# Sliding-window attention and two MoE-style layers on one core: weight blocks converted in another order

## The chip, the core and the metric

The kernel runs on one core of one Trainium2 chip. The metric is the device time of one execution in microseconds (us). Five engines work side by side, each through its own instructions in order: TensorE (PE in the profile, its weight loads PEld), VectorE (DVE), ScalarE (ACT), GpSimd (POOL) and SyncE (SP), which here only issues the DMA transfers.

## What is computed

```python
x = attention(q, k, v)                 # 2 x 8 heads x 768 x 64, own window of 96 keys and 8 global keys
x = x.transpose(0, 2, 1, 3).reshape(1536, 512)
h = x @ w_in1                          # 512 x 2048
x = (max(h, 0) + alpha * min(h, 0)) @ w_out1
h = x @ w_in2
g = (a0 + a1*h + a2*h*h + a3*h*h*h) / (1 + |b0|*|h| + |b1|*h*h + 1e-6)
out = g @ w_out2                       # 1536 x 512, float32
```

q, k, v are float32; the four weight matrices and the coefficients arrive as float64.

## The kernel before

**Layers.** Each of the two layers works on three groups of 512 tokens (g = 0, 1, 2) and sixteen blocks of 128 inner units (fc or j = 0 to 15). A *step* is one group with one block: `first` (L663) multiplies the block of w_in with the group's x into a bank, `leaky` (layer one) or `rational_a` to `rational_h` (layer two) apply the activation, and `second` (L723) multiplies the result with the block of w_out and adds into banks 4 to 7, which hold the group's four sums of 128 tokens. Every operand is kept as a float32 high half and a low half (hi, lo), so each product is three: 12 matmuls of 128x512 in `first`, 12 in `second`.

**Order of the steps.** `plan_weights` (L214) writes the list of 96 steps by hand. Layer one: group 0, then 1, then 2 with the lower blocks 0 to 7 (steps 0 to 23), then the groups 0, 1, 2 with the upper blocks 8 to 15 (24 to 47). Layer two: the same, lower blocks in steps 48 to 71, upper ones in 72 to 95. So every group's sum is in two parts: after the lower blocks `drain` (L748) copies the four banks to `part` (or `first`) and saves them to DRAM, `fetch` (L771) brings them back, and after the upper blocks `drain` adds them to the banks on VectorE (L763). In layer one ScalarE then writes the new high half of x (L768) and VectorE, a little later, the low half (L769).

**Slots.** Slot s issues `first(s)`, the activation of step s-1 and `second(s-2)`. Slots 0 to 15 (`joint_slot`) stand beside attention: each also carries two of its 48 pieces (`half`, `before`), and there `second` is one slot nearer. From slot 16 (LATE) on, `plain_slot` (L812) has the layers alone. Every slot calls `tick` twice, so half-slots are numbered 2s and 2s+1.

**Conversion of weights.** 64 jobs (two layers, sixteen blocks, "in" and "out") each turn 128x512 float64 values into hi and lo. A job goes through `tick` (L266) in three half-slots: SP has loaded the doubles into one of four `stage` tiles; ScalarE scales the upper word into `de` (L303); in the next half-slot VectorE joins the bits in three passes (L290, L291, L292) into `dx`, after which SP may load the next stage; in the one after that ScalarE casts the high half (L278) and VectorE subtracts it for the low half (L281). That subtraction is put into the list of the next job's three passes at the third place, in the same half-slot as the cast:

```python
        if split:
            self.join.insert(min(2, len(self.join)), split)
```

The half-slot in which a job starts is a table of numbers. Before, the eight lower blocks of layer one start in half-slots -10 to 12, beside attention; the sixteen jobs of the upper ones in 33 to 55 and the 32 of layer two in 57 to 126, two of every three half-slots up to 96 and then every sixth.

**Where blocks live.** Beside attention there is room for four blocks (`early`); the lower eight go through these four slots, are spilled to DRAM (`spill`, L202, the pair of DMAs of a job at L206) and reloaded (`reload`, L211). When attention is done its memory becomes twelve further slots, so that all sixteen blocks have one. SP issues everything in program order: tokens, weights, spills, reloads, saved sums and output; one that waits holds all behind it.

## Time and profile before

| | |
|---|---|
| three runs | 703.98 us median (702.05 to 704.06) |
| the profiled execution | 702.31 us, span 700.4 us |
| busy in the span | PE 653.3, PEld 509.9, DVE 542.2, ACT 379.4, POOL 226.2 us |
| matmuls | 3250 records in the trace |
| DMA | 78.62 MB, mean 112 GB/s |

The span runs from the first to the last instruction; the rest of an execution's time lies around it. Busy time is that of one engine; a matmul's end is modelled, so the starts of products tell more than their durations. A row of a timeline has its start and its duration in us, the engine, the line, and in brackets the idle time ahead of it with what ended it.

### The profile page before, as it was taken

To read this page: it belongs to the slowest core of one execution; us is meant where nothing else is said; L and a number is where in the kernel's file an instruction comes from. 1 tells how busy PE (TensorE), PEld (TensorE's weight loads), DVE (VectorE), ACT (ScalarE), POOL (GpSimd) and SP (SyncE) were. 2 spreads that over 40 slices of the span, in tenths; PEclk is the share of its full clock that TensorE was granted. 3 is DMA by queue.
4 is the path that set the end of the run, shared out by engine and by line. 5 is a ranking of instruction groups with operands and counts; after the bars stand their busy time and mean duration, and the time that the engine had idled before them with its cause. 6 is when DMAs were issued, how large, how long until landed. Compare 5 with 4: busy or idle time off the path is not lost. (4 is left out here: it accounts for less than half of the span.)

```text
span 700.4 us, 9637 instructions
## 1 busy us (share of the span) xinstructions
PE 653.3 (93%) x3250; PEld 509.9 (73%) x3250; DVE 542.2 (77%) x980; ACT 379.4 (54%) x775; POOL 226.2 (32%) x327
## 2 busy tenths in 40 slices
PE   7988898999999999998898996999999999999995
PEld 6656666767777886776676774887878888888784
DVE  4787888634324888889888889999998788797885
ACT  3876565454433334333334237677777676576662
POOL 4785474445442222211112121222212222132221
PEclk8999899999999999999999998999999999999999
DMA  8996778734335435453353151013010030120301
GB/s 164 199 230 180 241 242 249 190 128 124 99 126 178 145 114 172 129 180 90 117 162 113 44 167 59 32 30 91 0 61 1 0 121 0 46 76 0 121 0 65
DMA packets 82554, 78.62 MB, mean 112 GB/s; under 512 B 45056, under 2 KB 61696, under 8 KB 82496
## 3 DMA queue, kind: packets, MB, share of 16 engines
q1 hardware_dynamic: 82496, 77.92, 38.1%
q8 instruction: 27, 0.44, 0.3%
q14 instruction: 31, 0.25, 0.1%
HBM read 58.11 MB, written 17.83 MB: 108 GB/s over the span
## 5 line engine op out<-in xcount | busy, mean ns | idle before, releaser
L679 POOL TENSOR_TENSOR glo<-act,ghi 128x512 fp32r<-128x512 f32 x48 | 64.8, 1349 | 215.0 <-ACT ghi L678 215.0
L721 POOL TENSOR_TENSOR glo<-act,ghi 128x512 fp32r<-128x512 f32 (+1 forms) x49 | 63.7, 1300 | 206.5 <-ACT ghi L717 188.5
L678 ACT CAST ghi<-act 128x512 fp32r<-128x512 f32 x48 | 29.8, 620 | 142.5 <-DVE act L677 131.4
L670 PE MATMUL bank<-xhi,winhi_f 128*128 128x512 f32 x256 | 68.4, 389 | 0.0
L670 PE MATMUL bank<-xhi,winlo_f 128*128 128x512 f32 x256 | 68.4, 389 | 0.0
L670 PE MATMUL bank<-xlo,winhi_f 128*128 128x512 f32 x256 | 68.4, 389 | 0.0
L676 DVE TENSOR_SCALAR act<-bank,al 128x512 f32<-128x512 f32 x48 | 35.8, 746 | 28.7 <-PE bank L670 28.7
L292 DVE SCALAR_TENSOR_TENSOR dx<-stage,dx 128x512 int32<-128x512 int32 x64 | 56.1, 876 | 1.1
L422 ACT ACTIVATE prob<-prob,stat 128x232 f32<-128x232 f32 (+1 forms) x96 | 44.8, 470 | 20.8 <-DVE stat L415 18.5
L670 PEld LDWEIGHTS bank<-xhi,winhi_f 128*128 128x128 f32 x256 | 48.1, 188 | 10.0
L670 PEld LDWEIGHTS bank<-xhi,winlo_f 128*128 128x128 f32 x256 | 48.1, 188 | 10.0
L670 PEld LDWEIGHTS bank<-xlo,winhi_f 128*128 128x128 f32 x256 | 48.1, 188 | 10.0
L434 POOL TENSOR_SCALAR prob<-prob,rec 128x232 f32<-128x232 f32 (+1 forms) x96 | 47.5, 506 | 18.5 <-DVE rec L429 14.7
L688 ACT ACTIVATE stage<-bank 128x512 f32<-128x512 f32 (+1 forms) x49 | 28.8, 588 | 40.2 <-PE bank L670 40.1
L291 DVE SCALAR_TENSOR_TENSOR dx<-de,dx 128x512 int32<-128x512 int32 x64 | 48.6, 759 | 2.2
L736 PE MATMUL bank<-ghi,wouthi_f 128*128 128x512 f32 x112 | 37.1, 422 | 12.7 <-ACT ghi L678 7.5
L415 DVE CUSTOM_DVE_ANT_0 prob<-bank,bm 128x232 f32<-128x232 f32 (+1 forms) x96 | 32.5, 374 | 19.5 <-PE bank L406 19.5
L717 ACT CAST ghi<-act 128x512 fp32r<-128x512 f32 (+1 forms) x49 | 30.2, 616 | 32.1 <-DVE act L714 32.1
L697 DVE SCALAR_TENSOR_TENSOR stage<-stage,abs_b 128x512 f32<-128x512 f32 (+1 forms) x49 | 36.1, 737 | 14.0 <-ACT stage L689 14.0
L736 PE MATMUL bank<-wouthi_f,ghi 128*128 128x512 f32 x144 | 42.2, 394 | 0.8 <-ACT ghi L717 0.8
L303 ACT ACTIVATE de<-stage 128x512 f32<-128x512 f32 x64 | 42.1, 670 | 1.1 <-DMA stage<-in_moe_w_out_dram 1.1
L736 PE MATMUL bank<-wouthi_f,glo 128*128 128x512 f32 x144 | 41.8, 392 | 0.8 <-POOL glo L721 0.7
(202 smaller groups left out, 1540.5 us busy)
## 6 DMA issues: line engine op xcount, KB each, us to landing
stage<-in_moe_w_in_dram SPq DMA_DIRECT2D x32, 512.0 KB, 4.3
stage<-in_moe_w_out_dram SPq DMA_DIRECT2D x32, 512.0 KB, 3.9
part<-saved_f SPq DMA_DIRECT2D x24, 256.0 KB, 4.3
saved_f<-part SPq DMA_DIRECT2D x20, 256.0 KB, 2.5
va<-in_v_dram SPq DMA_DIRECT2D x13, 256.0 KB, 5.9
out_dram<-part SPq DMA_DIRECT2D x11, 256.0 KB
rawk<-in_k_dram SPq DMA_DIRECT2D x10, 256.0 KB, 5.2
rawq<-in_q_dram SPq DMA_DIRECT2D x10, 256.0 KB, 5.7
```

What stands on the lines that cost most here:

```text
L291: lambda: nc.vector.scalar_tensor_tensor(y, e, -(2**31), y, ALU.bitwise_and, ALU.bitwise_or),
L292: lambda: nc.vector.scalar_tensor_tensor(y, low, 29, y, ALU.logical_shift_right, ALU.bitwise_or),
L303: nc.scalar.mul(self.de[n % 2], self.staged(n)[:, :, :, 1].bitcast(F32), 2.0**-112)
L415: nc.vector.tensor_tensor_reduce(p[:, j, :w], banks[pair[j]][:, :w], bm[:, 2 * c + j, :], 1.0, 3.0e38, ALU.add, ALU.min, st[:, j : j + 1])
L422: nc.scalar.activation(p[:, j, :w], p[:, j, :w], AF.Exp, bias=st[:, j : j + 1], scale=-1.0, accum_out=st[:, 2 + j : 3 + j])
L434: nc.gpsimd.tensor_scalar(p[:, j, :w], p[:, j, :w], r[:, j : j + 1], 1.0, ALU.mult, ALU.mult)
L670: nc.tensor.matmul(bk, w["in", a][:, c, :], x[:, c, :], start=e == 0, stop=e == len(seq) - 1)
L676: nc.vector.tensor_scalar(t, h, 0.0, self.al[:, fc : fc + 1], ALU.min, ALU.mult)
L679: nc.gpsimd.tensor_tensor(lo, t, hi.bitcast(F32), ALU.subtract)
L697: nc.vector.scalar_tensor_tensor(w, w, self.ab[:, 0:1], ab, ALU.add, ALU.mult)
L721: nc.gpsimd.tensor_tensor(lo, u, hi.bitcast(F32), ALU.subtract)
L736: nc.tensor.matmul(y[d], lhs, rhs, start=begin and e == 0, stop=last and e == 2)
```

## The change

In layer one group 2, and in layer two group 1, now take all sixteen blocks in one run, so that their sums are never saved, fetched or added; layer one's order becomes 0, 1 (lower), 2 (all), 0, 1 (upper), layer two's 2, 0 (lower), 1 (all), 2, 0 (upper). `drain` then casts group 2's high half straight from the bank and subtracts right behind it. The table of starts changes: the sixteen jobs of layer one's upper blocks start in every second half-slot from 15 to 45; the 32 of layer two in 24 half-slots of 48 to 93 (48, 50, 52, 54, 55, 56, 58, 60, 62, 68, 70, 71, 72, 74, 76, 78, 83, 84, 86, 87, 89, 90, 92, 93) and in eight from 101 to 136, five apart. The jobs of blocks 8 to 11, which start beside attention, have no slot yet: their halves go to `part[1]` and `part[2]`, are spilled from there, and come back by `reload` in slots 18 to 21. The low half's subtraction is kept in a list of its own and issued at the start of the next `tick`. `spill` is called in every `tick` that casts. `fetch` looks one step further ahead.

```diff
@@ tables
+KEPT = CH + 4
+SAVED = ((0, 0), (0, 1), (1, 2), (1, 0))
...
@@ arm
-            self.spilled = [self.alloc_slot(spill, i, "d") for i in range(CH)]
+            self.spilled = [self.alloc_slot(spill, i, "d") for i in range(KEPT)]
...
@@ spill
         while self.unspilled:
-            fc, kind, slot = self.unspilled.popleft()
-            for part in PARTS:
-                self.nc.sync.dma_start(out=words(self.spilled[fc][kind, part]), in_=words(self.slots[slot][kind, part]))
+            to, of = self.unspilled.popleft()
+            self.nc.sync.dma_start(out=to, in_=of)
@@ plan_weights
-        self.steps += [(0, 2, fc, fc) for fc in range(CH)]
-        self.steps += [(0, g, fc, fc) for g in range(NGR) for fc in range(CH, NF)]
-        self.steps += [(1, g, j, j) for half in range(2) for g in range(NGR) for j in range(half * CH, (half + 1) * CH)]
+        self.steps += [(0, 2, fc, fc) for fc in range(NF)]
+        self.steps += [(0, g, fc, fc) for g in (0, 1) for fc in range(CH, NF)]
+        self.steps += [(1, g, j, j) for g in (2, 0) for j in range(CH)]
+        self.steps += [(1, 1, j, j) for j in range(NF)]
+        self.steps += [(1, g, j, j) for g in (2, 0) for j in range(CH, NF)]
...
+        spare = [(fc, kind) for fc in range(CH, NF) for kind in ("in", "out")]
+        for t, (fc, kind) in enumerate(spare):
+            jobs[2 * (CH + t) - 1] = 0, fc, kind, None if fc < KEPT else fc
...
-        times = [t for t in range(2 * LATE, 2 * layer) if t % 3 < 2] + list(range(2 * layer, 2 * (layer + half), 6))
+        times = [t for t in range(48, 96) if (t % 2 == 0 or t in (55, 71) or t > 82) and t not in (64, 66, 80, 82, 85, 88, 91, 94, 95)]
+        times += range(101, 160, 5)
@@ tick
+        while self.splits:
+            self.splits.popleft()()
         self.join_step(5)
-        split = None
         if self.pipe and self.pipe[0][0] == "joined":
...
+            self.spill()
+            x = words(self.dx[n % 3])
+            if slot is None:
+                hi, lo = (t.bitcast(F32R) for t in self.part[1:3])
+            else:
+                hi, lo = (flat(self.slots[slot][kind, part]) for part in PARTS)
...
-            split = lambda: nc.vector.tensor_sub(lo, x, hi.bitcast(F32))
-            self.spill()
-            if m == 0 and fc < CH:
-                self.unspilled.append((fc, kind, slot))
+            self.splits.append(lambda: nc.vector.tensor_sub(lo, x, hi.bitcast(F32)))
+            if m == 0 and fc < KEPT:
+                for part, of in zip(PARTS, (hi, lo)):
+                    self.unspilled.append((words(self.spilled[fc][kind, part]), of.bitcast(F32)))
...
-        if split:
-            self.join.insert(min(2, len(self.join)), split)
@@ drain
-            else:
-                xh, xl = self.xhi[g][:, d, :], self.xlo[g][:, d, :]
+            xh, xl = self.xhi[g][:, d, :], self.xlo[g][:, d, :]
+            if n in self.adds:
                 nc.scalar.copy(xh, o)
                 self.later.append(lambda: nc.vector.tensor_sub(xl, o, xh.bitcast(F32)))
+            else:
+                nc.scalar.copy(xh, y)
+                nc.vector.tensor_sub(xl, y, xh.bitcast(F32))
@@ plain_slot
-            fetch(s)
+            fetch(s + 1)
+            if CH <= s - LATE + CH - 2 < KEPT:
+                self.reload(s - LATE + CH - 2)
```

In the fences below `act` is the activation's tile, `de`, `dx` and `stage` those of a conversion, `winlo`, `wouthi` and the like the halves of a block; a line number is that of the kernel it comes from. First VectorE in slot 37 and the head of slot 38, layer one without attention. Before:

```order
L676 TENSOR_SCALAR act_99<-bank_82,al 128x512
L677 SCALAR_TENSOR_TENSOR act_99<-bank_82,act_99 128x512
L290 TENSOR_SCALAR dx_97<-de_95 128x512
L291 SCALAR_TENSOR_TENSOR dx_97<-de_95,dx_97 128x512
L281 TENSOR_TENSOR winlo_f<-dx_96,winhi_f 128x512
L292 SCALAR_TENSOR_TENSOR dx_97<-stage_93,dx_97 128x512
L281 TENSOR_TENSOR woutlo_f<-dx_97,wouthi_f 128x512
L676 TENSOR_SCALAR act_100<-bank_83,al 128x512
L677 SCALAR_TENSOR_TENSOR act_100<-bank_83,act_100 128x512
```

The same piece in the changed kernel:

```order
L696 TENSOR_SCALAR act_99<-bank_82,al 128x512
L697 SCALAR_TENSOR_TENSOR act_99<-bank_82,act_99 128x512
L303 TENSOR_TENSOR woutlo_f<-dx_97,wouthi_f 128x512
L303 TENSOR_TENSOR winlo_f<-dx_98,winhi_f 128x512
L312 TENSOR_SCALAR dx_96<-de_95 128x512
L313 SCALAR_TENSOR_TENSOR dx_96<-de_95,dx_96 128x512
L314 SCALAR_TENSOR_TENSOR dx_96<-stage_91,dx_96 128x512
L696 TENSOR_SCALAR act_100<-bank_83,al 128x512
L697 SCALAR_TENSOR_TENSOR act_100<-bank_83,act_100 128x512
```

Before, a low half stood among or behind passes of the half-slot of its own cast. Now each stands at the head of a half-slot, ahead of the three passes, and belongs to a cast of the half-slot before.

Second, ScalarE in slot 11, beside attention (`pt` is the copy of transposed probabilities, `x` a block of attention's result, `prob` the exponentials). Before:

```order
L678 CAST ghi_102<-act_100 128x512
L450 COPY pt_253<-bank_83 128x512
L470 COPY x_1_256<-bank_84 128x512
L422 ACTIVATE prob_243,stat_248<-prob_243,stat_248 128x232 x2
L450 COPY pt_254<-bank_83 128x512
```

In the changed kernel:

```order
L698 CAST ghi_102<-act_100 128x512
L300 CAST part_76<-dx_97 128x512
L323 ACTIVATE de_94<-stage_90 128x512
L470 COPY pt_267<-bank_83 128x512
L490 COPY x_1_270<-bank_84 128x512
L442 ACTIVATE prob_257,stat_262<-prob_257,stat_262 128x232 x2
```

A job's cast into `part[1]` (part_76) and the next job's scaling now stand between ghi and the copies.

Third, SP in the same slot of the changed kernel, where before only reloads stood:

```order
L216 DMA winhi__115<-dwinhi_f 128x512
L216 DMA winlo__116<-dwinlo_f 128x512
L216 DMA wouthi__117<-dwouthi_f 128x512
L216 DMA woutlo__118<-dwoutlo_f 128x512
L268 DMA stage_93<-in_moe_w_out_dram 128x1024
L211 DMA dwinhi_f<-part_76 128x512
L211 DMA dwinlo_f<-part_77 128x512
```

A load of weights and the spill of the job before, out of `part[1]` and `part[2]`, follow the four reloads.

## Rows read from the trace of the kernel before

**Rows 1.** Chain of waits, near its end: start, us, what.

```profile
528.06 2.72 PE bank L670 x12
530.78 2.72 PE bank L736 x12
```

**Rows 2.** Timeline of TensorE: first products of slots 17, 51, 95; second of step 48.

```profile
219.06 1.07 PE L670 MATMUL bank<-xhi,winhi__115 128*128 128x512 f32 x4
...
433.43 0.79 PE L736 MATMUL bank<-wouthi__113,ghi 128*128 128x512 f32 x1 [5.61 <-ACT ghi L717]
...
438.71 1.38 PE L670 MATMUL bank<-xhi,winhi__123 128*128 128x512 f32 x4
...
681.27 1.07 PE L670 MATMUL bank<-xhi,winhi_f 128*128 128x512 f32 x4
```

**Rows 3.** Busy by stretch: us; PE, PEld, DVE, ACT, POOL; clock, DMA share, GB/s.

```profile
143.54:208.90 65.36, 63.86 (x414) 47.67 (x412) 22.14 (x74) 28.47 (x79) 29.63 (x57) 1.00 0.39 125
...
219.06:438.71 219.65, 198.61 (x817) 154.04 (x816) 192.96 (x272) 88.95 (x153) 44.94 (x33) 0.98 0.41 128
```

**Rows 4.** Groups of VectorE from 219.06 to 438.71: busy, mean ns | idle ahead.

```profile
L292 DVE SCALAR_TENSOR_TENSOR dx<-stage,dx 128x512 int32<-128x512 int32 x43 | 39.2, 912 | 0.8
L291 DVE SCALAR_TENSOR_TENSOR dx<-de,dx 128x512 int32<-128x512 int32 x43 | 32.7, 761 | 1.5
...
L281 DVE TENSOR_TENSOR winlo_f<-dx,winhi_f 128x512 fp32r<-128x512 f32 x18 | 18.4, 1022 | 4.5 <-ACT winhi_f L278 4.5
L290 DVE TENSOR_SCALAR dx<-de 128x512 int32<-128x512 int32 x43 | 17.9, 415 | 0.0
L281 DVE TENSOR_TENSOR woutlo_f<-dx,wouthi_f 128x512 fp32r<-128x512 f32 x17 | 17.3, 1015 | 14.8 <-ACT wouthi_f L278 14.8
...
L763 DVE TENSOR_TENSOR part<-bank,part 128x512 f32<-128x512 f32 x12 | 7.4, 676 | 0.0
```

**Rows 5.** Timelines of GpSimd and VectorE in slots 37 to 39.

```profile
343.55 1.30 POOL L679 TENSOR_TENSOR glo<-act,ghi 128x512 fp32r<-128x512 f32 x1 [5.73 <-ACT ghi L678]
...
344.03 1.37 DVE L281 TENSOR_TENSOR woutlo_f<-dx,wouthi_f 128x512 fp32r<-128x512 f32 x1 [1.28 <-ACT wouthi_f L278]
...
352.62 0.69 DVE L281 TENSOR_TENSOR woutlo_f<-dx,wouthi_f 128x512 fp32r<-128x512 f32 x1 [0.69 <-ACT wouthi_f L278]
...
355.80 1.67 DVE L292 SCALAR_TENSOR_TENSOR dx<-stage,dx 128x512 int32<-128x512 int32 x1
```

**Rows 6.** Busy by stretch of 10 us, around two ends of groups.

```profile
320.00:330.00 10.00, 7.53 (x30) 5.28 (x29) 8.62 (x14) 5.49 (x10) 1.36 (x2) 1.00 0.24 70
...
430.00:440.00 10.00, 6.57 (x17) 5.18 (x18) 9.82 (x15) 7.79 (x15) 2.70 (x2) 0.66 0.00 0
```

**Rows 7.** Slots 53 to 61, layer two: the stretch, then groups of VectorE.

```profile
449.92:499.43 49.51, 49.26 (x218) 40.47 (x217) 46.30 (x67) 37.30 (x63) 11.66 (x9) 1.00 0.14 43
...
L714 DVE SCALAR_TENSOR_TENSOR act<-act,na,stage 128x512 f32<-128x512 f32 x9 | 6.8, 751 | 0.3
...
L281 DVE TENSOR_TENSOR winlo_f<-dx,winhi_f 128x512 fp32r<-128x512 f32 x2 | 2.8, 1420 | 1.1 <-ACT winhi_f L278 1.1
```

**Rows 8.** Slot 11: timelines; DMA issues (us to landing); SP's waits (total, times, longest).

```profile
173.33 0.16 DVE L429 RECIPROCAL rec<-rec 128x2 f32<-128x2 f32 x1
...
178.37 0.62 ACT L678 CAST ghi<-act 128x512 fp32r<-128x512 f32 x1 [3.51 <-DVE act L677]
179.79 0.58 ACT L450 COPY pt<-bank 128x512 f32<-128x512 f32 x1 [0.80 <-PE bank L442]
...
182.46 0.44 PE L460 MATMUL bank<-pt,va 128*64 128x128 f32 x4
...
dwinhi_f<-winhi__123 SPq DMA_DIRECT2D x2, 256.0 KB, 5.2
...
dwoutlo_f<-woutlo__126 SPq DMA_DIRECT2D x2, 256.0 KB, 3.3
...
SPq L211 <- PE bank L736: 27.1, 4, 7.5
```

More of the change, by code (lines that the diff above doesn't have):

```diff
@@ L93, in arm @@
         self.slots = list(self.early)
-        self.pipe, self.join, self.unspilled, self.later = deque(), deque(), deque(), deque()
+        self.pipe, self.join, self.unspilled, self.later, self.splits = (deque() for _ in range(5))
         self.loads = self.started = self.used = 0
@@ L97, in arm @@
         with tc.tile_pool(name="spill_" + sfx, bufs=1, space=DRAM) as spill:
-            self.spilled = [self.alloc_slot(spill, i, "d") for i in range(CH)]
-            self.saved = [[spill.tile([P, NC, DM], F32, name=f"saved{m}{g}_{sfx}") for g in range(NGR)] for m in range(2)]
+            self.spilled = [self.alloc_slot(spill, i, "d") for i in range(KEPT)]
+            self.saved = {mg: spill.tile([P, NC, DM], F32, name=f"saved{mg[0]}{mg[1]}_{sfx}") for mg in SAVED}
             with tc.tile_pool(name="at_" + sfx, bufs=1) as pool:
@@ L216, in plan_weights @@
         self.steps += [(0, 1, fc, fc % NEARLY) for fc in (*range(NEARLY, CH), *range(NEARLY))]
-        self.steps += [(0, 2, fc, fc) for fc in range(CH)]
-        self.steps += [(0, g, fc, fc) for g in range(NGR) for fc in range(CH, NF)]
-        self.steps += [(1, g, j, j) for half in range(2) for g in range(NGR) for j in range(half * CH, (half + 1) * CH)]
+        self.steps += [(0, 2, fc, fc) for fc in range(NF)]
[3 more added lines that the diff above has]
+        self.steps += [(1, g, j, j) for g in (2, 0) for j in range(CH, NF)]
+        runs = [s[:2] for s in self.steps]
+        self.begins = {n for n in range(len(runs)) if n == 0 or runs[n - 1] != runs[n]}
+        self.ends = {n - 1 for n in self.begins if n} | {len(runs) - 1}
+        self.saves = {n for n in self.ends if runs[n] in runs[n + 1 :]}
+        self.adds = {n for n in self.ends - self.saves if runs[n] in SAVED}
         jobs = {}
@@ L224, in plan_weights @@
         half, layer = NGR * CH, NGR * NF
-        todo = [(2 * (half + k), 2 * LATE, 0, CH + k, kind) for k in range(CH) for kind in ("in", "out")]
+        spare = [(fc, kind) for fc in range(CH, NF) for kind in ("in", "out")]
+        for t, (fc, kind) in enumerate(spare):
+            jobs[2 * (CH + t) - 1] = 0, fc, kind, None if fc < KEPT else fc
+        todo = []
         for n, free in ((0, LATE), (CH, layer - CH)):
@@ L588, in attention_any @@
         st = pool.tile([P, 4], F32, name="a_st")
-        self.first_saved = self.part
+        self.first_saved = [pool.tile([P, DM], F32, name=f"a_first{d}") for d in range(NC)]
         def transposed(dst, scale, nm, i):
@@ L743, in second @@
                     drains.append((n, d))
-        def opens(n):
-            return n % (NGR * NF) < NGR * CH
         def drain(n, d):
@@ L750, in drain @@
             y, o, r0 = banks[4 + d], self.part[d], g * GT + d * P
-            saved, out = self.saved[m][g][:, d, :], self.out[r0 : r0 + P, :]
-            if opens(n):
+            out = self.out[r0 : r0 + P, :]
+            if n in self.saves:
                 if n < LATE - 1:
@@ L755, in drain @@
                 (nc.vector.tensor_copy if d == 3 and m else nc.scalar.copy)(o, y)
-                nc.sync.dma_start(out=saved, in_=o)
+                nc.sync.dma_start(out=self.saved[m, g][:, d, :], in_=o)
                 return
@@ L762, in drain @@
                 return
[L763 removed]
+            if n in self.adds:
+                nc.vector.tensor_add(o, y, o)
+            elif m:
+                (nc.vector.tensor_copy if d == 3 else nc.scalar.copy)(o, y)
             if m:
                 nc.sync.dma_start(out=out, in_=o)
[L766 to L767 removed]
+                return
+            xh, xl = self.xhi[g][:, d, :], self.xlo[g][:, d, :]
+            if n in self.adds:
                 nc.scalar.copy(xh, o)
                 self.later.append(lambda: nc.vector.tensor_sub(xl, o, xh.bitcast(F32)))
+            else:
+                nc.scalar.copy(xh, y)
+                nc.vector.tensor_sub(xl, y, xh.bitcast(F32))
         def fetch(n):
[L772 removed]
+            if n in self.adds:
                 for d in range(4):
[L774 removed]
+                    nc.sync.dma_start(out=self.part[d], in_=self.saved[steps[n][:2]][:, d, :])
         def joint_slot(s, halves):
```

19 lines of the change are left out of this document (7 added, 12 removed).

## Prediction

> **What bounds the kernel now.** I call slot s the time from the start of step s's first-layer-half products to the start of the next step's. I read four views in this order. First the chain of waits: near its end nothing but TensorE stands in it, twelve products of 2.72 us and twelve more of 2.72 [rows 1]. So a slot in which nobody keeps TensorE waiting lasts 5.44 us, and that is the floor of all 80 steps after attention. Then the times at which slots 17, 51 and 95 start [rows 2]. Slots 17 to 50 take 438.71 - 219.06 = 219.65 us where 34 x 5.44 = 184.96 would do: **34.7 us are lost** there. Slots 51 to 94 take 242.56 where 44 x 5.44 = 239.36 would do: 3.2 us lost. Then the table of stretches [rows 3]: the 34.7 us fall where VectorE is busy 192.96 of 219.65 us, and beside attention, 143.54 to 208.90, TensorE is busy 63.86 of 65.36 while VectorE works only 22.14. Last, what VectorE does in the bad stretch [rows 4]: the passes that convert a block of weights (L290 to L292) stand there 43 times each, and the subtraction that makes the low half (L281) has idle time ahead of it, 14.8 + 4.5 us, that ends with ScalarE's cast of the high half. Busy and waiting together make 212 of 219.65 us: in slots 17 to 50 VectorE, not TensorE, sets the pace.
>
> **Blocks moved away from there.** 43 conversions join in slots 17 to 50 [rows 4]. By the new plan there are 31: seven of layer one (started from half-slot 33 to 45) and 24 of layer two; eight have gone to slots 7.5 to 14.5, one is joined just before slot 17, and three of the rest have moved past slot 51. One conversion costs VectorE 0.415 + 0.761 + 0.912 + 1.02 = 3.11 us [rows 4], so 12 x 3.11 = 37.3 us leave. Group 2 of layer one now accumulates over all sixteen blocks and its four additions of 0.676 go: 2.7 us more. VectorE's work in the stretch falls to 192.96 - 40.0 = 153 us, 32 under TensorE's 185. This term alone takes the bound away, so the removal of the ScalarE wait is not needed for it.
>
> **Low halves one point later.** The subtraction now opens the next half-slot, when the cast is long done; the 19.3 us of waiting go, and nothing waits for the low half that early (its product comes at least a half-slot later). What stays is a collision. Beside GpSimd's own subtraction (343.55 to 344.85) the low half took 1.37 us, alone 0.69; where another conversion pass came there instead, that one took 1.67 [rows 5]. So I count the collision, about 0.7 to 1.0 us a slot, as handed on and not as saved. The Trainium skill, SBUF — State Buffer, section "SBUF: two separate sides", says why: VectorE with two SBUF inputs and GpSimd share a port pair by an exclusive lock, and the loser blocks for the whole instruction; by that rule too the next such pass pays. Had the slow passes been a matter of the low half alone, layer two below would come out some 3 us better; layer one, at its floor either way, would not.
>
> **What is left of the 34.7.** One stall must stay: the end of layer one. Step 47's sums still have to be added to saved ones, and the first step of layer two needs three passes behind that on VectorE and a cast. After the last product: addition 0.68, one low half of x of the same size, three passes of about 0.75 [rows 7], cast 0.62 [rows 8]: 4.2 us, against 2.72 us of products that TensorE has in hand, so 1.5 us idle and the handoffs, say 2. Now it idles 5.61 us there and then runs a stretch in which the granted clock is 0.66 [rows 2, 6], between the levels of 1.2 and 2.4 GHz; the stretch from 320 to 330, with TensorE idle 2.5 us of it, kept 1.00 [rows 6], so I charge no drop. I add 1 us for slots 51 and 52 to catch up, and 1 for the eight blocks that the plan crowds into slots 41.5 to 46.5. There VectorE has, in seven slots (38.1 us), seven steps' activations of two passes, 1.4 together by the size of those in [rows 7], eight blocks of 2.5 to 3.1, four additions and four low halves: 9.8 + 20 to 25 + 5.4 = 35 to 40 us. A step's halves are wanted two slots after its first products end, 10.9 us for some 3 us of work, so a backlog of 2 us is swallowed. **Left: 4 us**, ends 1.5 and 15 (below). All other group ends should cost nothing once VectorE is on time, since an addition keeps pace with the four banks.
>
> **Layer two.** Nine steps with three blocks now take 46.30 us of VectorE in 49.51 [rows 7]. A block is 0.42 [rows 4], two passes of 0.69 as the undisturbed one [rows 5] and a low half of 1.42 [rows 7], 3.2 us, so a step alone is (46.3 - 9.7) / 9 = 4.07. The plan now puts two blocks in five slots, from 50.5 to 68, where it had one in three up to 63. GpSimd's subtraction falls beside the first half-slot's passes; so blocks that join in that half collide twice (4.2 us), the others not at all (2.5), and five slots hold 20.3 + 6.7 = 27.0 of 27.2 us, against 15.4 and 0.7 of waiting in 16.3 now. Equally tight, a few slots longer, with one set of additions and one of saves fewer: **+1 us**, ends -1 and +6 (20.3 + 8.4 if both kinds collide: 1.5 over, four times).
>
> **Beside attention.** Eight conversions enter slots 7.5 to 15. VectorE has room: 22.14 of 65.36 us [rows 3] plus 8 x 3.1 is 47. ScalarE's order is the risk. These blocks have no home yet, so all eight go through the same two tiles, part1 and part2, and the spill of one is issued only when the next is cast. Take slot 11. VectorE is through with the scores at 173.5 [rows 8]; the low half of the last block and the three passes of the next (2.5 us) end at 176; the load goes out, then the two spills, at about 176.8 (half a microsecond an issue, an estimate); a spill lands 3.3 to 5.2 us later [rows 8], at 180.1 to 182.0. The new cast could start at 179.0, behind ghi [rows 8], so it waits 1.1 to 3.0 us for its tile. With the cast and the scaling behind it, about 0.6 each, the copy of the transposed probabilities starts at 181.3 to 183.2 instead of 179.79 and ends 0.58 later; TensorE wants it at 182.46 [rows 8]. It idles 0 to 1.4 us a slot, in seven slots (the first cast finds its tile free): 0 to 10 us, below nothing excluded because no TensorE wait ends there now. I take 0.6 a slot, below the middle since a longer slot gives the spill more time: **+4 us**. Four reloads more in slots 18 to 21 are of blocks used from slot 24 and have 16 us in hand: nothing. The spills of saved sums and their fetches that go were off the path: nothing.
>
> **Sum.** The profiled execution took 702.31 us, of it 700.44 span. 702.31 - 34.7 + 4 + 1 + 4 = 676.6. The median of the runs, 703.98, is 1.7 above the profiled one, within their spread; I forecast **677**.
>
> **Rivals.** (a) *The crowd at the end of layer one.* The eight blocks bring the backlog back, the layer's end keeps its 10 us (5.61 idle, the slow clock, and its catching up) and 5 us go in slots 42 to 47. For it: the layer ends with 35 to 40 us of work in 38.1. Against: VectorE arrives with no backlog. 702.3 - 34.7 + 15 + 1 + 4 = 688. (b) *All goes well*: the spill lands early, the layer's end costs 1.5, layer two gains 1: 702.3 - 34.7 + 1.5 - 1 = 668. (c) *The spill's round trip sets the pace, slower than before.* SP works in order; it holds up to 7.5 us at a reload until TensorE is through with the slot's old block [rows 8]. If a spill stands behind such a hold, it goes out at 184.3, lands at 189.5, and the copy is ready at 191.3, 8.8 us late, seven times: 62 us, and the time is 702.3 - 34.7 + 5 + 62 = 735. It decides from (34.7 - 5) / 7 = 4.2 us a slot on. Against it: in the order the reload of a slot waits for products of the slot before, which are over when the spill's turn comes. The Trainium skill, DMA: Bandwidth & Descriptors, section "Rules for kernel authors", tells authors to issue a transfer early and wait for it late; this change does the opposite, and by that rule (c) or the dear end of the attention term is what to expect. (d) *The dear end*: 10 us beside attention and 6 in layer two, 702.3 - 34.7 + 4 + 6 + 10 = 688. (e) *It does not do what it says*: some other engine paces slots 17 to 50 as VectorE does now. ScalarE is busy 88.95 and GpSimd 44.94 of 219.65 us [rows 3], which all but excludes it: no change, 702.
>
> **Chances.** Forecast (671 to 683) 0.61, (a) 0.13, (b) 0.12, (c) 0.05, (d) 0.06, (e) 0.03. About 0.3% is what a measurement of this kernel can tell from no change. Faster: 0.92, same 0.03, slower 0.05. The range takes in (a), (b) and (d) with a little for the bounds: 667 to 691.
>
> **What would show it.** Right: slots 18 to 47 at 5.44 us, VectorE near 153 us in the stretch from slot 17 to 51, no idle time ahead of the low halves, one TensorE gap of about 2 us at the end of layer one and no low clock behind it; beside attention, casts into part1 that wait for a DMA, and slots of 9.3 to 10 us. Wrong: slots of 6 us from 42 on (a); slots of more than 10.7 us beside attention (d), of 13 and more (c); VectorE waiting or still full in slots 20 to 40, which would break the first term.

## The result, and the profile after

The changed kernel takes **681.16 us** (median of 4 runs, 679.83 to 683.6) against 703.38 for the kernel before beside it (4 runs): ratio **0.969**, 95% interval 0.9657 to 0.9723. The profiled execution took 679.83 us, 677.8 of it span. The forecast was 677 in a range of 667 to 691: the sign and the size came out as forecast, though not every term did. Of the 3.2 us between the sum (676.6) and the profiled time, 3.1 lie in one term; the rest cancels.

Where the time went, by the starts of slots in TensorE's timeline (slot 17 starts at 219.06 before [rows 2], at 224.89 after), in us of the profiled executions:

| stretch | before | after | difference | forecast |
|---|---|---|---|---|
| start to slot 8 | 143.54 | 142.30 | -1.24 | 0 |
| slots 8 to 16, beside attention | 75.52 | 82.59 | +7.07 | +4 |
| slots 17 to 50 | 219.65 | 189.98 | -29.67 | -30.7 |
| slots 51 to 94 | 242.56 | 243.82 | +1.26 | +1 |
| rest of the span | 19.17 | 19.16 | -0.01 | 0 |

The table of stretches of the changed kernel, of slots 8 to 15 (to 221.99), 17 to 50 and 51 to 94, then of ten microseconds at the end of layer one (us; PE, PEld, DVE, ACT, POOL; granted clock, DMA share, GB/s):

```profile
142.30:221.99 79.69, 72.32 (x445) 53.32 (x444) 45.38 (x109) 38.02 (x97) 36.31 (x59) 0.98 0.61 196
224.89:414.87 189.98, 187.39 (x818) 153.90 (x817) 160.72 (x220) 72.61 (x125) 44.27 (x33) 0.99 0.42 135
414.87:658.69 243.82, 241.74 (x1057) 197.93 (x1056) 214.86 (x307) 171.84 (x290) 59.63 (x45) 1.00 0.12 39
410.00:420.00 10.00, 9.25 (x34) 7.44 (x34) 9.83 (x15) 6.47 (x11) 3.27 (x2) 0.83 0.00 0
```

In the second line TensorE is busy 187.39 of 189.98 us, where it was 198.61 of 219.65 [rows 3]; VectorE fell from 192.96 to 160.72 us. Slots 19 to 49 all take 5.44 us, the floor. Only two slots lose anything: 18 with 7.08 and 50 with 8.78 us.

**The end of layer one.** TensorE's timeline, where before it idled 5.61 us [rows 2]:

```profile
410.75 1.20 PE L756 MATMUL bank<-wouthi__113,ghi 128*128 128x512 f32 x4 [1.77 <-ACT ghi L737]
...
413.16 1.91 PE L756 MATMUL bank<-wouthi__113,glo 128*128 128x512 f32 x4
414.87 1.42 PE L690 MATMUL bank<-xhi,winhi__123 128*128 128x512 f32 x4
```

The idle time is 1.77 us, as worked out (1.5 and the handoffs). But the clock fell behind it, to a mean of 0.83 in the ten microseconds above: the last four second products last 1.91 us instead of 1.07, and the twelve from 410.75 to 414.87 take 4.12 us instead of 2.72. I had charged no drop.

**Slot 18.** ScalarE, SP and TensorE:

```profile
226.64 0.32 SPq L211 DMA_DIRECT2D dwouthi_f<-part  x1
...
233.55 1.68 ACT L772 COPY part<-bank 128x512 f32<-128x512 f32 x3 [4.43 <-DMA dwouthi_f<-part]
...
234.18 1.59 PE L756 MATMUL bank<-ghi,wouthi__113 128*128 128x512 f32 x3 [0.71 <-ACT part L772]
```

The spill of the last block without a home is issued at 226.64, behind a row of reloads. It reads the very tile into which a drain of slot 18 must copy, so ScalarE stands 4.43 us and TensorE loses 1.64 us in that slot. My prediction didn't look there.

**Beside attention.** VectorE, SP, ScalarE and TensorE in slot 10, which took 11.79 us instead of 9.28:

```profile
162.38 0.69 DVE L303 TENSOR_TENSOR part<-dx,part 128x512 fp32r<-128x512 f32 x1
...
164.84 0.83 DVE L314 SCALAR_TENSOR_TENSOR dx<-stage,dx 128x512 int32<-128x512 int32 x1
...
165.74 0.38 SPq L268 DMA_DIRECT2D stage<-in_moe_w_in_dram  x1
166.17 0.51 SPq L211 DMA_DIRECT2D dwouthi_f<-part  x1
...
171.27 0.62 ACT L300 CAST part<-dx 128x512 fp32r<-128x512 f32 x1 [2.67 <-DMA dwouthi_f<-part]
172.35 0.57 ACT L470 COPY pt<-bank 128x512 f32<-128x512 f32 x1
...
173.06 0.32 PE L460 MATMUL bank<-part,prob 128*128 128x128 f32 x1 [1.67 <-ACT pt L470]
```

This is the chain the prediction described, and slot 10 is over the 10.7 us that it named as a sign of rival (d). The low half is done at 163.07, but its spill goes out at 166.17, because the next block's load stands ahead of it on SP and waits for the pass that ends at 165.67. The next cast waits 2.67 us for the tile, the copy of the probabilities stands behind the cast, and TensorE idles 1.67 us. Only every second cast waits like that (6.1 us in three waits, 0.8 in two short ones), but four waits of TensorE on this copy add up to 5.9 us, and the granted clock is 0.98 instead of 1.00.

**The low halves.** The waits of VectorE in slots 17 to 50 (who <- whom: us in total, times, longest):

```profile
DVE woutlo_f L303 <- ACT wouthi_f L300: 8.9, 5, 4.4
DVE winlo_f L303 <- ACT winhi_f L300: 3.5, 3, 1.6
...
DVE winlo__112 L303 <- ACT winhi__111 L300: 1.3, 1, 1.3
```

The two large groups fell only from 19.3 us [rows 4] to 12.4. With six blocks that have names of their own, like the last line (five waits of 1.3, one of 0.7), 19.6 us remain; counted like that, the kernel before has 22.8. I had written that this waiting goes. It doesn't, yet slots 19 to 49 lose nothing: the experiments had to say why.

### The profile page after: what moved, and what is told of

Read it like the earlier page. It is cut to its first block, busy times and chain, and to the rows that moved or that the text cites. A ratio compares the mean times of both kernels' runs of the same rounds, so it can differ in the third digit from the quotient of the medians.

```text
span 677.8 us, 9620 instructions
## 1 busy us (share of the span) xinstructions
PE 643.3 (95%) x3250; PEld 509.6 (75%) x3250; DVE 541.0 (80%) x972; ACT 376.0 (55%) x771; POOL 233.2 (34%) x327
## 5 line engine op out<-in xcount | busy, mean ns | idle before, releaser
L741 POOL TENSOR_TENSOR glo<-act,ghi 128x512 fp32r<-128x512 f32 (+1 forms) x49 | 65.3, 1333 | 201.8 <-ACT ghi L737 190.4
L698 ACT CAST ghi<-act 128x512 fp32r<-128x512 f32 x48 | 29.8, 621 | 131.7 <-DVE act L697 124.9
L313 DVE SCALAR_TENSOR_TENSOR dx<-de,dx 128x512 int32<-128x512 int32 x64 | 60.9, 951 | 2.2
L442 ACT ACTIVATE prob<-prob,stat 128x232 f32<-128x232 f32 (+1 forms) x96 | 44.8, 470 | 21.6 <-DVE stat L435 19.3
L454 POOL TENSOR_SCALAR prob<-prob,rec 128x232 f32<-128x232 f32 (+1 forms) x96 | 50.2, 535 | 18.5 <-DVE rec L449 15.2
L314 DVE SCALAR_TENSOR_TENSOR dx<-stage,dx 128x512 int32<-128x512 int32 x64 | 54.4, 850 | 2.2
L696 DVE TENSOR_SCALAR act<-bank,al 128x512 f32<-128x512 f32 x48 | 35.7, 745 | 15.1 <-PE bank L690 15.0
L756 PE MATMUL bank<-woutlo_f,ghi 128*128 128x512 f32 x144 | 41.0, 389 | 0.0
```

The source lines that it names most:

```text
L313: lambda: nc.vector.scalar_tensor_tensor(y, e, -(2**31), y, ALU.bitwise_and, ALU.bitwise_or),
L314: lambda: nc.vector.scalar_tensor_tensor(y, low, 29, y, ALU.logical_shift_right, ALU.bitwise_or),
L442: nc.scalar.activation(p[:, j, :w], p[:, j, :w], AF.Exp, bias=st[:, j : j + 1], scale=-1.0, accum_out=st[:, 2 + j : 3 + j])
L454: nc.gpsimd.tensor_scalar(p[:, j, :w], p[:, j, :w], r[:, j : j + 1], 1.0, ALU.mult, ALU.mult)
L696: nc.vector.tensor_scalar(t, h, 0.0, self.al[:, fc : fc + 1], ALU.min, ALU.mult)
L741: nc.gpsimd.tensor_tensor(lo, u, hi.bitcast(F32), ALU.subtract)
```

## The experiments

The stretches of all kernels, as above; "profiled" is the execution that they belong to.

| kernel | to slot 8 | 8 to 16 | 17 to 50 | 51 to 94 | profiled |
|---|---|---|---|---|---|
| before | 143.54 | 75.52 | 219.65 | 242.56 | 702.31 |
| changed | 142.30 | 82.59 | 189.98 | 243.82 | 679.83 |
| low half back | 144.41 | 84.30 | 197.37 | 250.36 | 697.33 |
| cast first | 143.84 | 84.75 | 196.87 | 248.67 | 695.11 |
| only the later low half | 143.25 | 75.54 | 205.17 | 240.49 | 685.06 |
| old table | 149.74 | 77.09 | 204.30 | 239.88 | 691.65 |
| old order | 143.92 | 84.10 | 187.40 | 245.61 | 682.12 |
| spill early | 142.20 | 76.22 | 186.79 | 245.61 | 671.61 |
| spill early, reloads later | 142.31 | 76.29 | 186.79 | 245.64 | 671.75 |
| even starts | 142.07 | 84.46 | 187.97 | 241.41 | 676.74 |
| odd starts | 142.22 | 84.27 | 187.99 | 245.64 | 681.42 |
| spill early and even starts | 143.69 | 76.27 | 187.10 | 241.42 | 669.13 |
| one block in two slots | 143.53 | 76.27 | 187.35 | 244.54 | 672.37 |

**Each part by itself.** First the changed kernel with the low half back in the half-slot of its cast:

```
-        while self.splits:
-            self.splits.popleft()()
...
-            self.splits.append(lambda: nc.vector.tensor_sub(lo, x, hi.bitcast(F32)))
+            split = lambda: nc.vector.tensor_sub(lo, x, hi.bitcast(F32))
...
+        if split:
+            self.join.insert(min(2, len(self.join)), split)
```

> The changed kernel with the low half put back into the half-slot of its cast. Theory (VectorE has room now): layer one stands at TensorE's floor with 29 us of VectorE to spare, so waits that come back are swallowed; slots 19 to 50 stay at 5.44 us and the time at 680 to 683. Rival (the later low half is what freed TensorE): slots of 5.8 us and more come back in layer one, 690 or more.

Measured: 697.50 us (697.33 to 697.71), ratio 0.9923 (0.99 to 0.9946), 16 us above the changed kernel. **My theory fell.** VectorE is as little loaded as in the changed kernel (158.09 us in slots 17 to 50), and still those slots take 7.4 us more, 3.6 of it in slots 30 to 33. Against the kernel before, the other two parts take 22.3 us off these slots, but 8.8 come on beside attention and 7.8 in layer two.

The other way round, the kernel before with nothing but the later low half:

```
...
+        while self.splits:
+            self.splits.popleft()()
         self.join_step(5)
-        split = None
...
-            split = lambda: nc.vector.tensor_sub(lo, x, hi.bitcast(F32))
+            self.splits.append(lambda: nc.vector.tensor_sub(lo, x, hi.bitcast(F32)))
...
-        if split:
-            self.join.insert(min(2, len(self.join)), split)
```

> The kernel before with the later low half alone; order of steps and table of starts as before. Theory: VectorE is full there, 19 of its 212 us are that wait, so nearly all of it comes off the time: 684 to 691. Rival (in a full VectorE the wait turns up ahead of the next pass instead): under 5 us, 698 or more.

Measured: 690.59 us (685.06 to 692.47), ratio 0.9833 (0.9798 to 0.9868): 13 us come from this alone. The theory held. Slots 17 to 50 fall from 219.65 to 205.17 us with all 43 conversions still in them (the profiled execution is the fastest of the four, 5.5 us under the median).

The changed kernel with the table of starts of before, no block without a home, so nothing more beside attention:

```
-KEPT = CH + 4
+KEPT = CH
...
-        for t, (fc, kind) in enumerate(spare):
-            jobs[2 * (CH + t) - 1] = 0, fc, kind, None if fc < KEPT else fc
-        todo = []
+        todo = [(2 * (half + k), 2 * LATE, 0, CH + k, kind) for k in range(CH) for kind in ("in", "out")]
...
+            if s == CH + 1:
+                self.spill()
...
```

> The changed kernel with the table of starts of before: nothing of the upper blocks beside attention, 43 conversions in slots 17 to 50; order of steps and later low half as in the change. Theory (the move of blocks is needed to get to the floor): beside attention the 7 us come back, layer one loses some 15 us to a VectorE with 190 us and its collisions, 685 to 692. Rival (the other two parts would have been enough): under 680.

Measured: 684.78 us (683.11 to 691.65), ratio 0.9738 (0.9714 to 0.9763), just under the expectation. (The profiled run is the slowest; its extra 7 us lie before slot 0, so I compare stretches.) The new table wins 14.3 us in slots 17 to 50 (204.30 against 189.98) and pays 5.5 beside attention and 3.9 in layer two: 3.6 us of net gain in the medians. That made the two payments the place to look.

The changed kernel with the order of the steps of before:

```
...
-        self.steps += [(0, 2, fc, fc) for fc in range(NF)]
-        self.steps += [(0, g, fc, fc) for g in (0, 1) for fc in range(CH, NF)]
+        self.steps += [(0, 2, fc, fc) for fc in range(CH)]
+        self.steps += [(0, g, fc, fc) for g in range(NGR) for fc in range(CH, NF)]
...
```

> The changed kernel with the order of steps of before: every group's sum in two parts, six saves and six additions instead of four; table and low half as in the change. Theory (additions are 2.7 us each layer on a VectorE that has room): 680 to 684. Rival (fewer ends of groups is what counts): each end costs 2 to 5 us as it did before, 686 or more.

Measured: 681.92 us (681.27 to 682.64), ratio 0.97 (0.9675 to 0.9724). Doing both halves of a group's inner units in one run is worth under 1 us here, no more than the scatter of the two kernels; the extra saves and additions cost next to nothing.

**What the later low half does.** VectorE's timeline tells it. I call the time from one slot's activation to the next one's VectorE's round. A block that is started in an odd half-slot, in slots 18 to 24; first the changed kernel, one slot (L696, L697 the activation, L303 the low half, L312 to L314 the passes):

```profile
243.91 0.75 DVE L696 TENSOR_SCALAR act<-bank,al 128x512 f32<-128x512 f32 x1
...
245.30 0.68 DVE L303 TENSOR_TENSOR woutlo_f<-dx,wouthi_f 128x512 fp32r<-128x512 f32 x1
245.90 0.42 DVE L312 TENSOR_SCALAR dx<-de 128x512 int32<-128x512 int32 x1
246.35 1.68 DVE L313 SCALAR_TENSOR_TENSOR dx<-de,dx 128x512 int32<-128x512 int32 x1
248.06 0.69 DVE L314 SCALAR_TENSOR_TENSOR dx<-stage,dx 128x512 int32<-128x512 int32 x1
248.67 0.74 DVE L696 TENSOR_SCALAR act<-bank,al 128x512 f32<-128x512 f32 x1
```

Then the kernel with the low half back (L697, L698 the activation, L302 the low half, L311 to L313 the passes):

```profile
251.19 0.74 DVE L697 TENSOR_SCALAR act<-bank,al 128x512 f32<-128x512 f32 x1
...
252.57 0.42 DVE L311 TENSOR_SCALAR dx<-de 128x512 int32<-128x512 int32 x1
253.02 0.69 DVE L312 SCALAR_TENSOR_TENSOR dx<-de,dx 128x512 int32<-128x512 int32 x1
253.75 1.66 DVE L313 SCALAR_TENSOR_TENSOR dx<-stage,dx 128x512 int32<-128x512 int32 x1
256.09 0.69 DVE L302 TENSOR_TENSOR winlo_f<-dx,winhi_f 128x512 fp32r<-128x512 f32 x1 [0.69 <-ACT winhi_f L299]
256.70 0.74 DVE L697 TENSOR_SCALAR act<-bank,al 128x512 f32<-128x512 f32 x1
```

VectorE's round takes 248.67 - 243.91 = **4.76 us** with the later low half and 256.70 - 251.19 = **5.51** without. TensorE needs 5.44. The collision with GpSimd, whose subtraction runs from 246.19 to 247.48 in the first of them, is in both (1.68 and 1.66 us instead of 0.69); what went is the wait of 0.69. A block that is started in an even half-slot, in slots 25 and on, in the changed kernel:

```profile
274.02 0.74 DVE L696 TENSOR_SCALAR act<-bank,al 128x512 f32<-128x512 f32 x1
...
276.77 1.36 DVE L303 TENSOR_TENSOR woutlo__114<-dx,wouthi__113 128x512 fp32r<-128x512 f32 x1 [1.29 <-ACT wouthi__113 L300]
...
279.84 0.74 DVE L696 TENSOR_SCALAR act<-bank,al 128x512 f32<-128x512 f32 x1
```

Here VectorE has nothing between the activation and the low half, "one point later" or not; the cast stands on ScalarE behind the cast to ghi (the activation's high half), and that waits for the activation. The round is **5.82 us** in this kernel, and with the low half back it is too (5.83, from 308.84 to 314.67). So the changed kernel can win 5.44 - 4.76 = 0.68 us a slot in the odd stretch and spends 0.38 a slot in the even one. What it has in hand can be read off: the time from the end of a step's ghi to the first of its second products that take it. For step 24, where the even stretch begins, in the changed kernel and then with the low half back:

```profile
269.76 0.62 ACT L698 CAST ghi<-act 128x512 fp32r<-128x512 f32 x1 [4.04 <-DVE act L697]
...
278.25 1.07 PE L756 MATMUL bank<-ghi,wouthi_f 128*128 128x512 f32 x4
```

```profile
280.09 0.62 ACT L699 CAST ghi<-act 128x512 fp32r<-128x512 f32 x1 [4.04 <-DVE act L698]
...
281.93 1.07 PE L757 MATMUL bank<-ghi,wouthi_f 128*128 128x512 f32 x4
```

In the changed kernel this lead grows from 4.26 us at step 18 to 278.25 - 270.38 = 7.87 at step 24, falls by 0.39 in each even round behind it and is 1.09 us, its least, at step 46: TensorE never sees the rounds that are too long. With the low half back it is 1.42 us at step 18 and 281.93 - 280.71 = 1.22 at step 24, and it is used up at step 27; from there TensorE waits, and slots 30 to 33 take 25.39 us, 21.76 in the changed kernel. Of the 6.65 us between the two leads at step 24, 3.8 come from the odd rounds. The other 2.8 are there at step 18 already, behind the stall of slot 18: where its drain holds up ScalarE, one low half waits 6.2 us with the low half back and 4.4 in the changed kernel. No run has the low half back without that stall, so how much of the 7.4 us would be left then is open.

To test that the wait comes from the order behind ghi, I put the block's work ahead of the activation, in the kernel with the low half back:

```
-            if ready and not steps[early][0]:
-                leaky(early)
             self.tick(True, 2 * s in self.starts)
+            if ready and not steps[early][0]:
+                leaky(early)
```

> The run with the low half back in its cast's half-slot, with one order changed: in a slot of layer one the block's cast and low half are now issued ahead of the step's activation instead of behind it. The same instructions, the same low half in the same half-slot as the cast. Theory: slots 31 to 34 took 5.8 to 7.0 us there because the cast stood behind ghi on ScalarE, which waits for the activation, and VectorE stood 1.28 us at the low half; ahead of ghi the cast finds ScalarE idle, the wait goes, and slots 31 to 34 and 42 return to 5.44 to 5.5 us, 4 to 5 us less in slots 17 to 50. Layer two and the attention are as in that run, so the whole lies at 692 to 694. Rival: it is the collision with GpSimd (1.37 instead of 0.69 us), not the wait; the collision stays, with the low half or with another pass, and the run stays at 696 to 698.

(The slots named there are counted one too high: they are 30 to 33 and 41.) Measured: 694.87 us (694.25 to 700.04), ratio 0.9894 (0.9837 to 0.9951), between theory and rival. Its timeline has the two kinds of block exchanged, an odd one in the first line, an even one in the others:

```profile
250.41 1.37 DVE L302 TENSOR_TENSOR woutlo_f<-dx,wouthi_f 128x512 fp32r<-128x512 f32 x1 [1.28 <-ACT wouthi_f L299]
...
312.22 1.67 DVE L313 SCALAR_TENSOR_TENSOR dx<-stage,dx 128x512 int32<-128x512 int32 x1
314.58 0.69 DVE L302 TENSOR_TENSOR woutlo__126<-dx,wouthi__125 128x512 fp32r<-128x512 f32 x1 [0.69 <-ACT wouthi__125 L299]
```

The even one now waits 0.69 us, its collision has moved to a pass, its round is 5.53 (activation at 310.44 and at 315.97), and slots 30 to 33 fall to 23.44 us. The odd one stands 1.28 us behind ghi, and slots 19 to 24, which were at the floor, take 5.8 us each. So order decides the wait, and wait and collision together make the round too long. With the collision and no wait it is the 4.76 us of the changed kernel's odd round. The wait of 1.28 without the collision was not run; worked out it would be 5.82 - 0.7 = 5.1 us, also under 5.44.

**What the attention pays.** The changed kernel with the spill issued right behind the low half:

```
         while self.splits:
             self.splits.popleft()()
+            self.spill()
...
             m, fc, kind, slot = self.plan[n]
-            self.spill()
```

> The changed kernel with one thing moved: the two spills of a block without a home are issued right behind its low half, ahead of the next block's load, and no longer when the next block is cast. Nothing else is different, the same conversions stand beside attention. Theory: the 7.0 us that slots 8 to 16 lost are the round trip of the spill, which SP holds behind the load, and the load waits for the conversion passes; with the spill out 2.5 us sooner the casts into part1 wait no more for a DMA (now 6.9 us in 5 waits), slots 8 to 16 fall from 79.7 to 75 or 76 us and the whole to 676 to 678. Rival: the engine work of eight more blocks costs it by itself; then the waits for the DMA shrink, slots 8 to 16 stay at 78 us or more, and the whole at 680 to 682.

Measured: **672.02 us** (671.33 to 675.56), ratio 0.9573 (0.9538 to 0.9608): 9 us, more than expected. SP's timeline with the early spill:

```profile
162.49 0.52 SPq L211 DMA_DIRECT2D dwouthi_f<-part  x1
...
165.53 0.38 SPq L268 DMA_DIRECT2D stage<-in_moe_w_in_dram  x1
```

The spill goes out at 162.49, ahead of the load, 3.7 us sooner. TensorE's waits from slot 8 to 17 (total, times, longest), in the changed kernel:

```profile
PE bank L460 <- ACT pt L470: 5.9, 4, 1.7
```

and with the early spill:

```profile
PE bank L460 <- ACT pt L470: 1.5, 1, 1.5
```

One wait of 1.5 us is left, which the kernel before has too. Slots 8 to 16 take 76.22 us: of the +7.07 that eight conversions cost there, 6.4 were SP's order and 0.7 the work. Slot 18 is back at the floor as well. Slot 50 takes 7.27 instead of 8.78 us, mainly because the clock did not fall there; it fell in slot 52 instead (last section).

The same with two reloads taken out of the row before slot 17:

```
...
-            if CH <= s - LATE + CH - 2 < KEPT:
-                self.reload(s - LATE + CH - 2)
+            if CH - 2 <= s - LATE + CH - 3 < KEPT:
+                self.reload(s - LATE + CH - 3)
...
-            for fc in range(NEARLY, CH):
+            for fc in range(NEARLY, CH - 2):
```

> As the run with the earlier spill, and the last two of the eight reloads that are issued in a row before slot 17 (blocks 6 and 7) go out in slots 17 and 18 instead, so that the last spills are less far back in SP's row. Theory: slot 18 loses 1.64 us because the spill of the last block without a home stands behind sixteen reloads and holds the tile that the first drain needs; the slot falls to 5.5 us, and the whole lies 1 to 1.6 us under the run with the earlier spill alone. Rival: the earlier spill mends slot 18 already, and this run equals that one within 0.5 us.

Measured: 672.43 us (671.75 to 673.29), ratio 0.9567 (0.9544 to 0.9591). The rival holds: once the spill is out early there is nothing left in slot 18 for the reloads to delay.

**What layer two pays.** Two kernels that differ from the changed one in one line, and from each other in parity alone:

```
-        times += range(101, 160, 5)
+        times += range(102, 150, 6)
```

> The changed kernel, with the last eight blocks of layer two started every sixth half-slot from 102 on, always at an even one, instead of every fifth from 101. Theory: in the changed kernel a block that joins in the first half of a slot meets GpSimd's subtraction once (a pass of 1.5 to 1.7 us instead of 0.69 to 0.75) and one that joins in the second half does not; with even starts none meets it, slots 51 to 94 lose 0.5 to 1.5 us where they now lose 4.5, and the whole is 677 to 679. Rival, density: two blocks in five slots or three in nine is no matter of collisions, a slot with a block and its leaky passes is simply late now and then: the loss shrinks with the number of blocks a slot, 4.5 x 5/6 = 3.7, and the whole stays at 680 to 681.

The odd one has `range(101, 149, 6)`.

> As the run with even starts, but every sixth half-slot from 101 on, always an odd one. The two runs have the same number of blocks in the same number of slots. Theory: every block meets GpSimd's subtraction, so slots 51 to 94 lose more than with even starts, 4 to 6 us, and the whole is 680 to 683, 3 us or more above the run with even starts. Rival, density: the two runs agree within 1 us.

Measured: even 676.97 us (676.38 to 678.17), ratio 0.9632 (0.9607 to 0.9656); odd 681.39 (678.71 to 681.87), ratio 0.968 (0.965 to 0.9711). Layer two loses 2.05 us with even starts (0.5 to 1.5 expected) and 6.28 with odd ones (4 to 6 expected), and the density is the same: the collisions make the difference. VectorE's groups from slot 51 to 94 (busy, mean ns | idle ahead), even:

```profile
L313 DVE SCALAR_TENSOR_TENSOR dx<-de,dx 128x512 int32<-128x512 int32 x8 | 5.5, 693 | 0.3
L314 DVE SCALAR_TENSOR_TENSOR dx<-stage,dx 128x512 int32<-128x512 int32 x8 | 5.5, 692 | 0.3
```

odd:

```profile
L313 DVE SCALAR_TENSOR_TENSOR dx<-de,dx 128x512 int32<-128x512 int32 x8 | 9.4, 1179 | 0.3
L314 DVE SCALAR_TENSOR_TENSOR dx<-stage,dx 128x512 int32<-128x512 int32 x8 | 8.5, 1058 | 0.3
```

Same instructions, same count, 6.9 us apart over eight blocks. The Trainium skill, SBUF — State Buffer, section "SBUF: two separate sides", has the port pair that VectorE and GpSimd share as the only place on the engine side of SBUF where one engine holds up another; this pair of runs agrees and puts a price on it, 0.9 us of VectorE a block. TensorE feels it in a few slots only. Slot 52 alone makes 2.6 of its 4.2 us, even first, then odd:

```profile
419.96:426.48 6.52, 5.73 (x25) 4.43 (x24) 6.35 (x11) 4.03 (x8) 1.31 (x1) 1.00 0.27 80
```

```profile
419.98:429.10 9.12, 7.25 (x26) 5.49 (x25) 8.91 (x14) 6.24 (x11) 1.63 (x1) 0.82 0.20 57
```

With odd starts TensorE waits 1.87 us in that slot instead of 0.79, and the granted clock falls behind it (0.82 over the slot), so 1.5 of the 4.2 us are the clock's (TensorE is busy 7.25 us with products that took 5.73).

**Both together**, the early spill and the even starts:

> The earlier spill and the even starts of layer two together. They touch different stretches, so if both explanations stand the gains add: the earlier spill gave 9 us and the even starts 4, and this run lies at 667 to 669 us; slots 51 to 94 lose about 2 us, as with even starts alone. Rival: with the earlier spill the layer's end came out differently (slots 50 and 52 took 7.27 and 9.21 us, with a granted clock of 0.66 behind slot 52's wait), so what is won early is paid there, and this run stays at 670 to 672.

Measured: **669.69 us** (6 runs, 667.22 to 671.56), ratio **0.9507** (0.947 to 0.9545), the fastest kernel here, faster than both, if just above the 667 to 669 expected. Each gain shows in its own stretch (76.27 and 241.42 us); in the medians 2.3 of the 4 us of the even starts arrive. The stretch to slot 8, which the even starts don't touch, took 143.69 us in this profile and 142.07 to 143.92 in the others of the changed kernel's code there (the old table's left out), so in the profiles 1.5 us of the gain are lost to that scatter.

Last, the early spill with the crowd at the end of layer one spread out:

```
-        times = [t for t in range(48, 96) if (t % 2 == 0 or t in (55, 71) or t > 82) and t not in (64, 66, 80, 82, 85, 88, 91, 94, 95)]
-        times += range(101, 160, 5)
+        times = [t for t in range(48, 96) if (t % 2 == 0 or t in (55, 71)) and t not in (64, 66, 80, 82) and t < 82]
+        times += range(84, 148, 4)
...
```

> The earlier spill, and the eight blocks that the change crowds into half-slots 83 to 93 together with the last eight spread as one block in two slots, at half-slots 84, 88 and so on to 144, all even. Theory: the stalls in slots 50 and 52 are the crowd, because VectorE comes to the first step of layer two with passes still to do; with three blocks in slots 42 to 47 instead of eight only about 1 us is left at slot 50 and none at 52, and the clock stays at 1.00; layer two has one block in two slots, none of them in collision, (3.4 + 0.7 beside attention's end) 2 x 4.07 + 2.5 = 10.6 of 10.88 us of VectorE, so it loses 1 to 2 us: 665 to 667 in all. Rival: the stalls are the layer's end itself (additions, low halves, three passes of the first step, 4.2 us against 2.72 of products) and stay at 2 to 4 us, and the denser layer two loses more than with one block in three slots: 668 to 671.

Measured: 672.56 us (6 runs, 671.28 to 675.05), ratio 0.9561 (0.9525 to 0.9598), above even the 668 to 671 of the rival, whose stalls are there. Its timelines of VectorE and TensorE at the end of layer one:

```profile
397.48 2.73 DVE L781 TENSOR_TENSOR part<-bank,part 128x512 f32<-128x512 f32 x4 [2.71 <-PE bank L756]
...
404.28 1.20 PE L756 MATMUL bank<-wouthi__113,ghi 128*128 128x512 f32 x4 [2.08 <-ACT ghi L737]
411.48 1.20 PE L756 MATMUL bank<-wouthi__117,ghi 128*128 128x512 f32 x4 [1.45 <-ACT ghi L737]
```

VectorE waits 2.71 us for TensorE ahead of the additions, so it carries no backlog, and TensorE still idles 2.08 us behind them. So the stall is the layer's end itself. Slots 51 to 94 take 3 us more than with one block in three slots, 1.8 of it in slot 51.

## Why the prediction was right, and where it was not

- *Forecast and sign*: right; 681.16 in 667 to 691. Worked on the profiled execution, 676.6 against 679.83. That the loss in slots 17 to 50 is 5.0 us for 4 forecast is partly luck: slot 18 (1.64) and the clock (1.4) were put at nothing, the 1 us for the crowd did not come, and the catching up (1.0 in slots 51 and 52) lies in the next stretch.
- *Moving twelve conversions and four additions out of slots 17 to 50*: VectorE's busy time fell by 32.2 us, not 40.0. The durations of all its instructions fell by 35.2: the 31 conversions left cost 3.24 us each where the 43 cost 3.10, and 32 low halves stayed, not 31. The other 3 us are overlap (passes of 0.69 us start 0.61 to 0.73 apart), which a sum of durations does not see. TensorE's pace came out as forecast.
- *"This term alone takes the bound away, so the removal of the ScalarE wait is not needed for it"*: **this step failed.** Without the later low half the time is 697.50. Of the 22 us the later low half brings 13 by itself and 16 on top of the other two parts; the new table brings 3.6 on top of the others, the new order under 1. I compared VectorE's sum over 34 slots, 153 us, with TensorE's 185. But VectorE works in order, and a round of activation, wait, low half and passes is 5.5 to 5.8 us in a slot that has a block, whatever the average. The sum came out right because the change had both parts; for this term that is luck.
- *"The 19.3 us of waiting go"* and *"no idle time ahead of the low halves"*: wrong: 12.4 of those 19.3 us remain, 19.6 of 22.8 with the blocks that have names of their own. The waits go where the round would be too long without a lead to pay for it (odd blocks) and stay where they are paid out of a lead (even ones).
- *The collision as handed on, not saved*: right in layer one, every round shown has one. In layer two it was mis-sized: a block joining in the first half collides once and its low half does not (0.68 us a low half), where I counted twice, and blocks that join in the second half hardly collide at all. That the stretch took 1.26 us more, near the 1 I gave, is in part luck: with the same density the starts alone move it from 2.05 to 6.28 us of loss. Twice is what the kernel with the low half back shows, which takes 6.5 us more there: in slots 51 to 94 its four low halves of "out" blocks take 1.42 us each and wait 2.2 us in all, 5.2 us of VectorE more than in the changed kernel. That these make most of the 6.5 us is likely, but no run takes them away by themselves.
- *The end of layer one*: 1.77 us of idle time for 2 forecast; the clock's fall, 1.4 us, was ruled out and came. The crowd, rival (a), costs nothing that can be seen: the lead is still 1.09 us at its least, and taking the crowd away left the stall.
- *Beside attention*: +7.07 for +4, with the mechanism and the chain as written. I took 0.6 us a slot, from a wait of 1.1 to 3.0; the longest were 2.67 and 2.45. What I didn't see is that it was avoidable: 6.4 of the 7.07 came back by one line. Rival (c) didn't occur. The Trainium skill, DMA: Bandwidth & Descriptors, section "Rules for kernel authors", wants a DMA that is to overlap with compute issued early and waited for late; the early spill agrees, with 9 us.
- *Slot 18*: I called the four late reloads nothing, which holds, but did not ask what the last spill stands behind: 1.64 us.
- *Saves and fetches that go: nothing*: right, the order of steps is worth under 1 us.

Not settled: whether anything else stands behind those 6.5 us, and why the part to slot 8 differs by up to 2 us between executions of the same code.

## What to carry to other kernels

Compare an engine's busy time with the bound slot by slot, not over the stretch: an in-order engine that waits once a slot for another that waits for it has a round of its own, and only the lead from easier slots can pay for it. Where a temporary must be spilled before it is used again, issue the spill when the data is ready, ahead of transfers that wait for something else. Where two engines hold each other up, as VectorE and GpSimd do here, the parity of a start can matter: 4.4 us with the same number of starts.

## What the runs showed of the hardware

The fall of TensorE's clock did not follow the length of the idle time before it. After 1.77 us in the changed kernel it fell (0.83 above); with odd starts after 1.76 us at the same place it stayed at 1.00, and fell after 1.87 us in slot 52. With the low half back it stayed at 1.00 after 2.45 and 2.47 us (slots 50 and 52), and with one block in two slots after 2.08 us:

```profile
400.00:410.00 10.00, 7.92 (x34) 5.93 (x32) 9.78 (x16) 6.66 (x12) 1.63 (x1) 1.00 0.02 4
```

With the early spill it kept 1.00 after 1.49 us in slot 50 and fell after 1.88 us in slot 52, where the second products took nearly double and the slot 9.21 us (TensorE, then a stretch of 5 us):

```profile
415.42 1.93 PE L756 MATMUL bank<-wouthi__121,ghi 128*128 128x512 f32 x4 [1.88 <-ACT ghi L737]
```

```profile
415.21:420.21 5.00, 4.79 (x14) 3.79 (x15) 4.89 (x9) 3.83 (x8) 1.62 (x1) 0.66 0.00 0
```

The twelve products took 4.12 us in the one case and 4.45 in the other instead of 2.72, so 1.4 to 1.7 us ride on such a gap. What decides is open here; a forecast should carry it as a chance, not leave it out. The slots beside attention scatter too while they wait for a transfer (82.59 to 84.46 us in four profiles) and stop once they do not (76.22 to 76.29 in four).
